# Declaring steps on different PSUM banks independent by part of a buffer instead of by whole buffer

## The chip, the cores and the metric

The kernel runs on one core of a Trainium2 chip. The metric is the device time of one execution in microseconds (us). A core has five engines that matter here, each with its own queue of instructions that it takes in order: PE (matrix products), DVE (elementwise work on vectors), ACT (activation functions and copies), POOL (elementwise work, without the accumulators) and SP (issues most DMAs). PE writes its results to PSUM, eight banks of 2 KB for each of 128 partitions; DVE and ACT read them from there. Engines wait for each other by semaphores.

## The reference

Two stages in one program. The first is a gated linear recurrence over 768 tokens for 4 batches of 8 heads of width 48, the second a feed-forward layer with the activation h * cos(h) on all 3072 tokens.

```python
f = 1.0 / (1.0 + np.exp(-f_logit))
for t in range(S):
    state = f[:, :, t, :, None] * state + np.einsum('bhd,bhe->bhde', k[:, :, t], v[:, :, t])
    y[:, :, t] = np.einsum('bhd,bhde->bhe', q[:, :, t], state)
x = np.ascontiguousarray(y.transpose(0, 2, 1, 3)).reshape(B * S, H * D)
h = x @ w_in                      # 384 -> 2048
out = (h * np.cos(h)) @ w_out     # 2048 -> 384
```

## The kernel before, in words

The tokens are cut into 12 pairs of two chunks of 128 tokens (three pairs a batch). For each pair n the recurrence is done in chunk form: the gates are made on ACT (steps ex, ln, fx, fy, lines 328 to 359), POOL and DVE scale queries and keys by the decays (qa, ka, qm, km, line 404 and before), PE makes running sums of log gates (cum, lines 374 and 380), products of queries and keys (sc, line 454; DVE masks them, am, line 458), and the products of keys and values for the carried state (ps, line 476; DVE adds the old state and scales, st at line 494 and sz at line 500). At last PE sums the outputs of the pair: y from masked products and values (`inner`, line 533) and yi from queries and carried state (`inter`, line 538), both with the matmul of line 528. The two chunks' outputs, py[0] and py[1], stand in one PSUM bank each.

The steps xe{n}.0 and xe{n}.1 (line 552) then copy the two banks to SBUF as bf16, each into its own half of one slot of the buffer x: `xg[g]` is a part of `x` (line 549). Which engine makes such a copy, ACT or DVE, is written down in the plan. The copies go through the helper of line 197, so the profile shows them as L197 with the tile x.

The feed-forward layer works in units of 128 or 256 tokens (13 units, `moe`, line 563). A unit of 256 tokens reads both halves of x: PE multiplies by w_in (h, line 576), ACT takes the cosine as a shifted sine from PSUM (co, line 581), DVE multiplies both into g (line 558), PE multiplies by w_out (o, line 592), ACT or DVE copies the result (ot) and a DMA stores it (out, line 603). The steps h{m} of unit m read x of pair m - 1 (units 0 and 1 both read pair 0).

The order of all steps is written out by hand in the table ORDER (line 36). A word such as `xe8.0:S1` names a step, its engine (T is PE, S is ACT, V is DVE, G is POOL, Y is SP) and the slots or banks that its new values get. `emit` (line 617) goes through the table and lets each step issue its instructions, so each engine's queue holds its steps in the order of the table. Semaphore waits are placed by the framework, which keeps instructions on one tile in order. PSUM is four tiles of two banks each (line 255), and for the framework a tile is one thing: instructions on its two banks are dependent unless told otherwise. That is what `apart` (line 642) does: it holds the last 12 steps on each PSUM tile (WITHIN, line 32) and declares a new step's instructions independent of an earlier step's on another engine if the steps touch no common bank and, by `places`, no common slot of any buffer in SBUF.

The two copies of a pair's x are such steps: their banks differ, but they lie in one tile in all pairs but the first, and both write the same slot of x. The words of the table for the pairs in which they stand on different engines of one tile: `xe1.0:V1 xe1.1:S`, `xe3.0:S1 xe2.1:S0 xe3.1:V xe2.0:V`, `xe6.1:S1 xe6.0:V`, `xe7.1:S0 xe7.0:V`, `xe8.0:S1 xe8.1:V`, `xe9.1:V2 xe9.0:S`, `xe11.0:V1 xe11.1:S`.

Of the kernel before, what the change touches and what calls it, by code (L numbers as in the profile page):

```python
# [616 lines left out]
def emit(tc, G, tiles):  # L617
    nc = tc.nc
    plan = []
    for word in ORDER.split():  # L620
        name, how = word.split(":")
        plan.append((G.steps[name], LETTER[how[0]], [int(x) for x in how[1:].split(",") if x]))
    assert len(plan) == len(G.steps)
    table, users = None, [[] for _ in tiles]
    for s, e, places in plan:
        for w in s.writes:
            v = w.whole
            if v.pool is not None and v.slot is None:
                v.slot = places.pop(0)
            w.first, w.final = not w.begun, w.left == 1  # L630
            w.begun, w.left = True, w.left - 1
        if s.table is not None:
            if s.table == "E" and table != "E":
                nc.scalar.preload_act_table_set("natural_log_exp_and_others")
            table = s.table
        n0 = nc.next_id()
        s.fn(e)
        made = (nc.find_inst_by_name(f"I-{i}") for i in range(n0 + 1, nc.next_id()))
        apart(tc, users, s, e, [i for i in made if i is not None])


def apart(tc, users, s, e, made):


    vals = [v.whole for v in s.reads + s.writes]
    banks = {b for v in vals if isinstance(v.pool, Banks) for b in range(v.slot, v.slot + v.pool.size)}
    places = {(v.pool.name, v.slot) for v in vals if v.pool is not None and not isinstance(v.pool, Banks)}
    for t in {b // 2 for b in banks}:
        for engine, others, theirs, there in users[t]:
            if engine != e and not banks & theirs and not places & there:  # L650
                for b in others:
                    for a in made:
                        tc.declare_no_dep(a, b, reason="the steps use different PSUM banks")
        users[t].append((e, made, banks, places))
        del users[t][:-WITHIN]


# [48 lines left out]
```

## Time and profile before

| what | value |
|---|---|
| median of 3 runs | 190.7 us (189.53 to 192.26) |
| the profiled execution | 189.83 us |
| its span, first to last instruction | 187.8 us |
| mean granted clock of PE | 0.991 |
| busy: PE, DVE, ACT, POOL | 175.9, 140.5, 134.4, 105.1 us |

The profile is that of one execution. A row of the timeline or of a group gives the start in us from the begin of the span, the length in us, the engine, the line of the kernel, the operation, what it writes and reads, and how many instructions are taken together; in square brackets stands the idle time of the engine just before, and what ended it. PEld is PE's loading of weights, which runs beside its matmuls. A row of the list of waits reads "who <- for whom: us in total, times, longest". In the rows of a tile the three numbers with slashes are the shortest, median and longest duration in ns. "The chain that ended last" is followed back from the last instruction, at each step to what released it. A merged row can overlap the next, since matmuls are pipelined and their ends are modelled.

### The profile page before, as it was taken

The page shows a single profiled execution, that of the slowest core. Times are in us where ns is not written, and L with a number is a line of the kernel's source. Part 1 is how long each engine was busy: PE and PEld are TensorE (multiplying, and loading weights), DVE is VectorE, ACT ScalarE, POOL GpSimd, SP SyncE. Part 2 cuts the span into 40 slices and gives each one's busy share as a digit, 9 for nine tenths or more (in the row PEclk, how much of TensorE's full clock was granted, in tenths as well). Part 3 has the DMA queues.
Part 4 walks back from the last instruction along what each step waited for, and adds up shares of the span by engine and source line. Part 5 has one row for each costly group of instructions (what it writes and reads, how often), then busy time and mean ns, then how long its engine had stood idle before and what let it go on. Part 6 is the DMA issues. An engine that isn't in the chain of part 4 may idle for free.

```text
span 187.8 us, 5973 instructions
## 1 busy us (share of the span) xinstructions
PE 175.9 (94%) x2540; PEld 125.8 (67%) x2540; DVE 140.5 (75%) x207; ACT 134.4 (72%) x193; POOL 105.1 (56%) x132
## 2 busy tenths in 40 slices
PE   7879877999999999999999999997999999999992
PEld 2345446886658876678767786665867876776661
DVE  5089869796697999999998889777999868335231
ACT  2798925997979999999999878688766573432310
POOL 3256787998548697998534979989960000000000
PEclk9999979999999999999999999999999999999999
DMA  5999999999927999976599997999581100111034
GB/s 126 268 198 266 365 358 324 280 291 251 268 43 197 231 289 186 266 186 128 108 205 256 263 248 135 171 254 224 131 196 43 47 0 0 45 42 42 0 129 168
DMA packets 72282, 33.94 MB, mean 181 GB/s; under 512 B 65344, under 2 KB 70720, under 8 KB 72256
## 3 DMA queue, kind: packets, MB, share of 16 engines
q1 hardware_dynamic: 68688, 32.09, 72.1%
q10 hardware_dynamic: 3568, 1.48, 3.3%
q8 instruction: 20, 0.33, 0.8%
q14 instruction: 6, 0.05, 0.1%
HBM read 25.17 MB, written 4.72 MB: 159 GB/s over the span
## 4 chain that ended last, share of the span: by engine, by line
PE 55%; DMA 11%; POOL 10%; ACT 9%; DVE 9%; issue 3%; SPq 1%; POOLq 0%; DVEq 0%; ACTq 0%
PE ps L592 24%; PE ps L576 23%; DMA f<-in_f_logit_dram 6%; POOL qk L404 4%; DMA k<-in_k_dram 3%; ACT co L581 3%; PE ps L454 3%; PE ps L528 3%; DVE am L458 3%; DMA out_dram<-ot 2%; POOL vb L197 2%; DVE qk L404 2%; POOL sp L363 2%; POOL vt L197 2%; DVE sz L500 2%
## 5 line engine op out<-in xcount | busy, mean ns | idle before, releaser
L558 DVE TENSOR_TENSOR g<-ps,co 128x1024 bf16<-128x1024 f32 x48 | 60.8, 1308 | 16.7 <-ACT co L581 16.0
L576 PE MATMUL ps<-x,w_in_bf 128*128 128x256 bf16 (+1 forms) x624 | 68.8, 266 | 3.0 <-ACT x L197 1.3
L581 ACT ACTIVATE co<-ps,halfpi 128x1024 bf16<-128x1024 f32 x48 | 52.3, 1115 | 23.6 <-PE ps L576 22.4
L592 PE MATMUL ps<-w_out_bf,g 128*128 128x384 bf16 x384 | 68.2, 326 | 0.0
L576 PEld LDWEIGHTS <-w_in_bf 128*128 128x128 bf16 x624 | 57.0, 99 | 11.9 <-issue 3.5
L592 PEld LDWEIGHTS <-g 128*128 128x128 bf16 x384 | 36.3, 98 | 21.3
L458 DVE TENSOR_TENSOR am<-ps,pmask 128x1024 bf16<-128x1024 f32 x24 | 28.9, 1219 | 6.0 <-PE ps L454 5.6
L404 POOL TENSOR_TENSOR qk<-k,bi 128x384 bf16<-128x384 f32 x22 | 21.9, 1003 | 0.9
L404 POOL TENSOR_TENSOR qk<-q,b 128x384 bf16<-128x384 f32 x21 | 20.8, 1000 | 1.0 <-ACT b L395 0.3
L363 POOL TENSOR_TENSOR sp<-ls 128x384 bf16<-128x384 f32 x10 | 10.0, 1000 | 13.2 <-ACT ls L333 10.5
L264 PE MATMUL ps<-zero 128*128 128x512 bf16 x50 | 14.9, 432 | 1.2 <-DVE zero L203 1.2
L197 POOL COPY vt<-vb 64x384 bf16<-64x384 bf16 x28 | 14.2, 509 | 1.9 <-ACT vb L197 0.5
L500 DVE TENSOR_TENSOR sz<-ps,b 64x192 bf16<-64x192 f32 x40 | 14.1, 354 | 1.2
L351 POOL TENSOR_TENSOR k<-k,f 128x384 f32<-128x384 f32 (+1 forms) x12 | 11.2, 932 | 5.2 <-DMA k<-in_k_dram 4.3
L494 DVE TENSOR_TENSOR ps<-ps,sz 64x192 f32<-64x192 f32 x32 | 11.7, 365 | 1.7 <-PE ps L476 0.7
L329 ACT ACTIVATE f<-f 128x768 f32<-128x768 f32 (+1 forms) x14 | 10.3, 746 | 2.8 <-DMA f<-in_f_logit_dram 2.2
L197 ACT COPY ot<-ps 128x384 f32<-128x384 f32 (+1 forms) x13 | 5.6, 438 | 8.3 <-PE ps L592 4.2
L197 DVE COPY ot<-ps 128x384 f32<-128x384 f32 (+1 forms) x13 | 6.8, 532 | 6.2 <-PE ps L592 2.9
L197 POOL CAST vb<-v 128x768 bf16<-128x768 f32 x9 | 7.3, 823 | 7.2 <-DMA v<-in_v_dram 7.2
L341 POOL TENSOR_TENSOR q<-f,q 128x384 f32<-128x384 f32 x10 | 9.9, 999 | 1.7 <-DMA q<-in_q_dram 1.5
L454 PE MATMUL ps<-qkt 48*64 48x128 bf16 x384 | 9.9, 225 | 0.5 <-DVE qkt L197 0.2
L197 ACT COPY vt<-vb 64x384 bf16<-64x384 bf16 x20 | 10.0, 507 | 0.3
(64 smaller groups left out, 167.1 us busy)
## 6 DMA issues: line engine op xcount, KB each, us to landing
out_dram<-ot SPq DMA_DIRECT2D x22, 192.0 KB, 2.3
f<-in_f_logit_dram SPq DMA_DIRECT2D x10, 384.0 KB, 5.9
v<-in_v_dram SPq DMA_DIRECT2D x10, 384.0 KB, 6.1
q<-in_q_dram SPq DMA_DIRECT2D x10, 384.0 KB, 5.3
k<-in_k_dram SPq DMA_DIRECT2D x10, 384.0 KB, 6.5
g<-in_moe_w_in_dram SPq DMA_DIRECT2D x4, 768.0 KB, 9.1
g<-in_moe_w_out_dram SPq DMA_DIRECT2D x4, 768.0 KB, 7.1
v<-in_v_dram ACTq DMA_DIRECT2D x2, 384.0 KB, 5.9
```

The lines of the kernel that those rows point to most:

```text
L197: (nc.scalar.copy if e == "ACT" else eng(e).tensor_copy)(out=o, in_=i)
L264: G.step(f"zf{i}", ("PE",), lambda e, dump=dump: nc.tensor.matmul(dump.ap, lhsT=zero[:, 0:128], rhs=zero, start=True, stop=True), writes=[ ...
L363: G.step(f"ad{n}", ("POOL",), lambda e: eng(e).tensor_add(out=sp.ap[:, 0, :, 0:D], in0=soft.ap[:, :, 0, :], in1=soft.ap[:, :, 1, :]), read ...
L404: G.step(f"{nm}{n}.{u}", ("POOL", "DVE") if cut else ("POOL",), lambda e, u=u, j=j, src=src, dec=dec: eng(e).tensor_mul(out=qkp[u][j].ap[: ...
L454: nc.tensor.matmul(o[t, r, 2 * a + g, :].rearrange("p (e n) -> p e n", e=2), lhsT=qkv(u)[s, 1, a, g, x, :], rhs=qkv(u)[s, 0, a, g, :, :], ...
L458: G.step(f"am{n}.{u}", ("DVE",), lambda e, u=u, sc=sc: nc.vector.tensor_mul(out=am[u].ap.rearrange("p r b n -> p (r b) n"), in0=sc.ap.rear ...
L494: nc.vector.tensor_add(out=view()[s], in0=view()[s], in1=S0.ap[s, :, r, :])
L500: eng(e).tensor_mul(out=new.ap[s, :, r, :].rearrange("p (u a) n -> p u a n", u=2), in0=view()[s].rearrange("p (u a) n -> p u a n", u=2), i ...
L558: nc.vector.tensor_mul(out=o.rearrange("p b (n e) -> p b e n", e=2), in0=ph.ap.rearrange("p (b e n) -> p b e n", e=2, n=64), in1=co.ap.rea ...
L576: nc.tensor.matmul(ph.ap[:, i * T:(i + 1) * T].rearrange("p (g t) -> p g t", t=C), lhsT=w_in_bf[:, kk, f0:f0 + 128], rhs=xa[:, :, kk, :], ...
L581: G.step(f"co{m}.{j}", ("ACT",), lambda e, ph=ph, co=co: nc.scalar.activation(out=co.ap, in_=ph.ap, func=AF.Sin, bias=halfpi), reads=[ph], ...
L592: nc.tensor.matmul(po.ap[:, 0:DM], lhsT=gT.ap[:, j, i * C:(i + 1) * C], rhs=w_out_bf[:, j, :], start=(po.first and j == 4 * s), stop=(po.f ...
```

## The change

Only `apart` is changed. In place of the set of slots that a step touches, it keeps for each value outside PSUM the value as named by the step (a whole or a part), the whole behind it, and if it is written. Two steps meet if one of them writes, both use the same slot of the same pool, and the values are in each other's way: different wholes in one slot (an old and a new occupant), the same part, or one of them the whole. Two different parts of one whole do not meet, nor do two reads. Steps on different banks that don't meet are declared independent.

```diff
-    places = {(v.pool.name, v.slot) for v in vals if v.pool is not None and not isinstance(v.pool, Banks)}
+    home = lambda v: v.whole.pool is not None and not isinstance(v.whole.pool, Banks)
+    uses = [(v, v.whole, i) for i, vs in enumerate((s.reads, s.writes)) for v in vs if home(v)]
+
+    def meet(theirs):
+        for v, w, wr in uses:
+            for v2, w2, wr2 in theirs:
+                if (wr or wr2) and w.pool is w2.pool and w.slot == w2.slot:
+                    if w is not w2 or v is v2 or v is w or v2 is w2:
+                        return True
+        return False
     for t in {b // 2 for b in banks}:
         for engine, others, theirs, there in users[t]:
-            if engine != e and not banks & theirs and not places & there:
+            if engine != e and not banks & theirs and not meet(there):
                 for b in others:
                     for a in made:
                         tc.declare_no_dep(a, b, reason="the steps use different PSUM banks")
-        users[t].append((e, made, banks, places))
+        users[t].append((e, made, banks, uses))
```

## The prediction

> **What bounds the kernel now.** I read the page first (busy shares, the slices, the shares of the chain that ended last), then the list of who waited for whom, then the rows of the tile x, and last the timeline around each copy that the change touches.
>
> ```profile
> span 187.8 us, 5973 instructions
> PE 175.9 (94%) x2540; PEld 125.8 (67%) x2540; DVE 140.5 (75%) x207; ACT 134.4 (72%) x193; POOL 105.1 (56%) x132
> ...
> PEclk9999979999999999999999999999999999999999
> DMA  5999999999927999976599997999581100111034
> ...
> PE 55%; DMA 11%; POOL 10%; ACT 9%; DVE 9%; issue 3%; SPq 1%; POOLq 0%; DVEq 0%; ACTq 0%
> ```
>
> PE is busy for 94% of the span at nearly full clock, and the chain that ended last runs mostly over PE. The DMA engines are full in most slices of the first three quarters, so POOL, which prepares each pair from loaded data, can hold PE up as well. From the list of waits, the rows that join the copies of x with anything:
>
> ```profile
> DVE x L197 <- ACT x L197: 3.3, 4, 1.6
> ACT x L197 <- DVE x L197: 3.1, 3, 1.7
> ...
> PE ps L576 <- ACT x L197: 1.3, 1, 1.3
> PE ps L576 <- DVE x L197: 1.0, 2, 0.6
> ...
> PE ps L576 <- DVE sz L500: 0.7, 2, 0.4
> ```
>
> Seven times the copy of one half of x on one of DVE and ACT waits for the copy of the other half on the other, 3.3 + 3.1 = 6.4 us together. PE stands at its first matmul of line 576 behind such a copy three times, 1.3 + 1.0 = 2.3 us. These 2.3 us, and whatever stands behind them, are all that the edit can give directly.
>
> ```profile
> L197 ACT CAST x<-ps x13: 478/478/485, 20.2 to 149.6; 128x384 bf16<-128x384 f32 x13
> L197 DVE CAST x<-ps x11: 539/558/558, 22.4 to 149.0; 128x384 bf16<-128x384 f32 x11
> ```
>
> **What changes.** Both built programs hold the same instructions in the same order on each engine; only waits differ. The halves xg[0] and xg[1] read two banks of one PSUM tile and write two parts of one slot of x. Before, the common slot kept them dependent; after, the parts are disjoint and the wait between them goes. That happens in pairs 1, 2, 3, 6, 7, 8, 9 and 11, where the steps xe stand on different engines. Pairs 4, 5 and 10 have both copies on one engine, and pair 0 has its two banks in different tiles. In return each copy waits for its own PE sums; and PE's first line-576 step after such a pair, which waited once (for the later copy), now waits twice: DVE's copy at the weight load, ACT's at the matmul. A few copies of line 197 and activations of line 581 also name DVE or PE work that they had covered through the other copy. That work has long ended when they are reached, so I take nothing for it.
>
> **Pair 1 (31 to 33 us).**
>
> ```profile
> 31.21 0.51 PE L528 MATMUL ps<-qkt,sz 128*32 128x128 bf16 x24
> ...
> 31.65 0.10 PEld L576 LDWEIGHTS <-w_in_bf 128*128 128x128 bf16 x1
> 31.92 0.54 DVE L197 CAST x<-ps 128x384 bf16<-128x384 f32 x1
> ...
> 32.49 0.48 ACT L197 CAST x<-ps 128x384 bf16<-128x384 f32 x1 [0.51 <-DVE x L197]
> ...
> 33.02 4.09 PE L576 MATMUL ps<-x,w_in_bf 128*128 128x256 bf16 x36 [1.30 <-ACT x L197]
> ```
>
> ACT is free from 32.49 - 0.51 = 31.98, and the sums end at 31.72. So ACT copies from 32.0 to 32.48 beside DVE (31.92 to 32.46). PE's weight load, done ahead at 31.65 before, now waits for DVE and takes 0.10 after it; the matmul starts at about 32.60 instead of 33.02. Gain 0.42. ACT goes on to its weight cast 0.5 us sooner; the activations behind it move with PE.
>
> The Trainium skill, TensorE: Matmul & The Clock Gate, section "Step-by-step: what each phase is for", says that PE draws weight loads ahead of matmuls still in flight. The trace agrees in the load at 31.65, 1.37 us ahead of its matmul. By that page's column rule a load that is not overlapped costs an estimated 128 / 1.2 = 107 ns, which speaks against this edit: eight loads would give back 0.85 us.
>
> By the row, eight loads would cost 8 x 0.10 = 0.8 us if PE stood idle at all eight. It stands idle at three, and at two of these ACT's copy ends last, so I charge it once, above.
>
> **Pair 6 (104 to 106 us).**
>
> ```profile
> 105.16 0.48 ACT L197 CAST x<-ps 128x384 bf16<-128x384 f32 x1
> 105.27 0.62 PE L528 MATMUL ps<-am,vt 128*32 128x128 bf16 x32
> 105.67 0.56 DVE L197 CAST x<-ps 128x384 bf16<-128x384 f32 x1 [0.89 <-ACT x L197]
> ...
> 106.28 8.02 PE L576 MATMUL ps<-x,w_in_bf 128*128 128x256 bf16 x72 [0.39 <-DVE x L197]
> ...
> 112.69 0.82 POOL L197 CAST vb<-v 128x768 bf16<-128x768 f32 x1 [1.22 <-DMA v<-in_v_dram]
> ...
> 115.21 1.96 POOL L404 TENSOR_TENSOR qk<-k,bi 128x384 bf16<-128x384 f32 x2
> 117.48 0.50 PE L476 MATMUL ps<-vb,qk 64*64 64x48 bf16 x28
> ```
>
> DVE's copy moves into its 0.89 us of waiting and is done before ACT's ends at 105.64; PE's own sums of pair 7 end at 105.89. So PE goes on at 105.89, 0.39 sooner. But at 117.48 PE takes ps9.1, which needs POOL's products, done at 115.21 + 1.96 = 117.17, and POOL had stood 1.22 us for a load of v. If that load lands when it did, only 117.48 - 117.17 = 0.31, less 0.04 for the signal (the step from the end of ACT's copy in pair 1, 32.97, to PE's start is 0.05), gets past this point: 0.27. The 0.42 of pair 1 must pass there too. Together the two are worth between 0 and 0.42 + 0.39 = 0.81; I take 0.27, since the load of v is the nearest row that decides it.
>
> **Pair 8 (126 to 131 us).**
>
> ```profile
> 125.99 0.51 PE L528 MATMUL ps<-qkt,sz 128*32 128x128 bf16 x24
> 126.83 0.31 PE L476 MATMUL ps<-vb,qk 64*64 64x48 bf16 x16
> 127.40 0.48 ACT L197 CAST x<-ps 128x384 bf16<-128x384 f32 x1
> 127.91 0.56 DVE L197 CAST x<-ps 128x384 bf16<-128x384 f32 x1 [1.57 <-ACT x L197]
> 128.38 0.35 DVE L494 TENSOR_TENSOR ps<-ps,sz 64x192 f32<-64x192 f32 x1
> 128.52 1.47 PE L576 MATMUL ps<-x,w_in_bf 128*128 128x256 bf16 x12 [0.62 <-DVE x L197]
> 128.65 1.21 DVE L458 TENSOR_TENSOR am<-ps,pmask 128x1024 bf16<-128x1024 f32 x1
> 129.92 0.63 PE L528 MATMUL ps<-am,vt 128*32 128x128 bf16 x32
> 130.30 0.74 DVE L500 TENSOR_TENSOR sz<-ps,b 64x192 bf16<-64x192 f32 x2
> 131.10 5.59 PE L576 MATMUL ps<-x,w_in_bf 128*128 128x256 bf16 x48 [0.38 <-DVE sz L500]
> ```
>
> ACT reaches its half late (127.40) and DVE, idle for 1.57 us, queued the carry st10, the mask am9.1 and the states sz10 behind its own. After, DVE copies once the sums end (126.50): 126.54 to 127.10. The carry needs ps10 (end 127.14): 127.18 instead of 128.38, 1.20 sooner, and am9.1 and sz10 with it (am9.1 ends at 128.66, sz10 at 131.04 - 1.20 = 129.84). PE starts h8.01 when ACT's copy ends, 127.88 + 0.04 = 127.92, not 128.52: 0.60. It is at y9 at 129.92 - 0.60 = 129.32, where am9.1 is ready, and reaches h8.30 at 131.10 - 0.38 - 0.60 = 130.12, where sz10 is ready too: the 0.38 goes as well. Gain 0.98, with 0.60 as its lower end, if something else takes the place of sz10.
>
> **The other pairs.**
>
> ```profile
> 57.87 0.56 DVE L197 CAST x<-ps 128x384 bf16<-128x384 f32 x1 [0.53 <-ACT x L197]
> 58.75 0.56 DVE L197 CAST x<-ps 128x384 bf16<-128x384 f32 x1 [0.33 <-ACT x L197]
> ...
> 132.07 0.48 ACT L197 CAST x<-ps 128x384 bf16<-128x384 f32 x1 [0.93 <-DVE x L197]
> ...
> 149.63 0.48 ACT L197 CAST x<-ps 128x384 bf16<-128x384 f32 x1 [1.70 <-DVE x L197]
> ```
> ```profile
> 58.54 7.97 PE ps L576 x72
> ...
> 175.19 9.11 PE ps L592 x56
> ```
>
> In pairs 2, 3, 9 and 11 a copy moves forward by up to 0.9 us, but PE is busy over all of them (58.54 to 66.51; 131.10 to 136.69; in pair 11 with the next unit's matmuls), so I take nothing. Without that cover each would give at most a copy, 0.5 us. Pair 7 shows no wait.
>
> **The sum.** 0.27 + 0.98 = 1.25 us, bounds 0.60 and 0.42 + 0.39 + 0.98 = 1.79. From 131 us to the output matmuls at 175.19 and on, PE has no listed idle, so what is won there should reach the end. The profiled execution took 189.83 us (span 187.8 and 2.0 around it), which gives 188.6. The median of the runs shown, 190.7, lies 0.9 above it and gives 189.45. I predict between them, 189.0.
>
> **Rivals.**
> 1. *The waits come back elsewhere.* PE gets to y9, to h8.30 or to ps9.1 sooner and stands there for POOL or a load. For it: full DMA slices and POOL's 1.22 us behind v. Against: the rows at 130.12 above, where the operands are ready. Worth 0 to 0.5, so about 190.4.
> 2. *Everything moves along*, the load of v too, since its issue hangs on POOL and SP work that hangs on PE: the full 1.79, about 188.4 against the middle of the two bases. Removing even all 2.3 us of waits listed stays below 2%.
> 3. *Slower: the weight loads.* If a load with a wait on it stops PE at all eight places, also where PE is not idle, that costs 0.8 us; it decides once less than 0.8 of the 1.25 is won. With the gain of rival 1 at nothing the time is 190.7 + 0.8 = 191.5. Against: DVE's copy has ended when PE comes to the load in pairs 2, 3, 7, 9 and 11.
> 4. *The two copies slow each other*, reading one PSUM tile at once. If each takes the sum, 0.48 + 0.56 = 1.04 us, nothing is won: 190.7. The trace has no such pair to show it; ACT's copy took 478 to 485 ns in all 13 cases, in some beside DVE reading another tile.
>
> The Trainium skill, PSUM — Partial Sum Buffer, section "Specifications (TRN2)", says that the two engines read PSUM in parallel at full speed where the banks differ. No run here shows that for one tile.
>
> That the edit does nothing is excluded by the differing waits.
>
> **Chances and range.** Forecast 0.60, everything moves along 0.12, waits come back 0.16, slower by the loads 0.08, copies slow each other 0.04. Two per cent, 3.8 us, is about what a measurement of this kernel can tell from no change: the runs before alone spread over 2.7 us. No case reaches it by its own arithmetic; leaving room for a timing effect that I do not see (loads that fall differently), I say 0.07 faster, 0.88 within, 0.05 slower. The range goes from the lowest run before less the upper bound, 189.53 - 1.79 = 187.7, a little lowered to 187.4, up to the slower rival, 191.5.
>
> **What would show it.** Right: no wait between ACT x and DVE x in the list; PE's idle at 33.02 down to about 0.9, those of pairs 6 and 8 gone, and that on sz10 gone; DVE's carry st10 straight after the sums of pair 8 and 10, some 1.2 us sooner than before. Wrong: a new PE idle time at 117 or 129 to 131 of the size of the gain, copies of x longer than 0.56 us, or weight loads of line 576 with idle time at the other pairs.

## The result, and the profile after

The changed kernel takes 188.7 us at the median of 21 runs (186.57 to 190.19), the kernel before 190.74 (188.65 to 192.53, 21 runs). The ratio is 0.9867, 95% interval 0.9839 to 0.9896: faster, by 2.0 us at the medians and by 2.0 to 3.1 us by the interval, and so by less than 2%. The ratio leaves out the slow runs of each kernel, those more than 1.5% above its fastest, which are 7 of the 21 of the changed kernel; so it shows more than the medians do. Forecast were 189.0 and no change over 2%.

In the profiled execution (189.68 us) PE's clock was low for longer in the first 31 us than in the profile before, as the clock row shows, so its span hardly shows the gain, and I compare stretches after that point instead. From its page:

```profile
span 187.5 us, 5972 instructions
PE 177.0 (94%) x2536; PEld 126.9 (68%) x2540; DVE 140.4 (75%) x207; ACT 134.3 (72%) x193; POOL 105.3 (56%) x132
...
PEclk9999957999999999999999999999999999999999
```

From the list of waits and the rows of the tile x of the same execution:

```profile
DVE x L197 <- PE ps L528: 1.8, 4, 0.6
ACT x L197 <- PE ps L528: 1.7, 3, 1.1
...
PEld L576 <- DVE x L197: 0.8, 1, 0.8
...
PE ps L576 <- ACT x L197: 0.7, 1, 0.7
```
```profile
L197 ACT CAST x<-ps x13: 470/478/486, 20.0 to 148.9; 128x384 bf16<-128x384 f32 x13
L197 DVE CAST x<-ps x11: 534/557/558, 22.5 to 148.9; 128x384 bf16<-128x384 f32 x11
```

The copies of x no longer wait for each other; they wait for PE's sums, as they should. Of PE's three waits for a copy at line 576 one is left, that of pair 1. The copies take as long as before, though they now run side by side on two banks of one tile. The timeline at the three places of the prediction:

```profile
32.33 0.51 PE L528 MATMUL ps<-qkt,sz 128*32 128x128 bf16 x24
32.89 0.56 DVE L197 CAST x<-ps 128x384 bf16<-128x384 f32 x1 [0.55 <-PE ps L528]
32.99 0.47 ACT L197 CAST x<-ps 128x384 bf16<-128x384 f32 x1
...
33.50 0.55 PEld L576 LDWEIGHTS <-w_in_bf 128*128 128x128 bf16 x6 [0.84 <-DVE x L197]
33.51 0.71 PE L576 MATMUL ps<-x,w_in_bf 128*128 128x256 bf16 x5 [0.68 <-ACT x L197]
```
```profile
105.97 0.56 DVE L197 CAST x<-ps 128x384 bf16<-128x384 f32 x1
...
106.36 0.48 ACT L197 CAST x<-ps 128x384 bf16<-128x384 f32 x1
...
107.02 1.70 PE L576 MATMUL ps<-x,w_in_bf 128*128 128x256 bf16 x14
```
```profile
118.56 0.50 PE L476 MATMUL ps<-vb,qk 64*64 64x48 bf16 x28 [0.25 <-POOL qk L404]
```
```profile
127.06 0.51 PE L528 MATMUL ps<-qkt,sz 128*32 128x128 bf16 x24
127.62 0.56 DVE L197 CAST x<-ps 128x384 bf16<-128x384 f32 x1 [0.21 <-PE ps L528]
...
128.33 0.36 DVE L494 TENSOR_TENSOR ps<-ps,sz 64x192 f32<-64x192 f32 x1
128.47 0.48 ACT L197 CAST x<-ps 128x384 bf16<-128x384 f32 x1
...
129.00 1.47 PE L576 MATMUL ps<-x,w_in_bf 128*128 128x256 bf16 x12
...
131.13 3.12 PE L576 MATMUL ps<-x,w_in_bf 128*128 128x256 bf16 x27
```

In pair 1 PE's idle falls from 1.30 to 0.68 us. In pair 6 and ahead of unit 8 the brackets are gone, and so is that on sz10. A new wait has come at ps9.1 (118.56), on POOL's qk, at the place that the prediction named. From the start of the sums yi8 to that of h8.30 it was 131.10 - 125.99 = 5.11 us before and is 131.13 - 127.06 = 4.07 now.

**The whole span in stretches.** ACT has the same instructions in the same order, all of them recorded, in every kernel here but the two that move a copy of pair 8. So I cut each execution at the starts of seven of them (before: co at 30.86, the load of a function table at 45.79, x at 105.16, co at 112.08, fx at 121.21, vt at 126.87, co at 136.73 us) and subtract. The stretch from 121.21 to 126.87 is 5.66 us in all of them and is left out. Below, `all` is the change once more; the other names are those of the experiments.

| execution | up to 30.86 | 31 to 46 (pair 1) | 46 to 105 | pair 6 | ps9.1 | pairs 8, 9 | to the end |
|---|---|---|---|---|---|---|---|
| before | 30.86 | 14.92 | 59.38 | 6.92 | 9.13 | 9.86 | 51.03 |
| base_look1 | 30.57 | 14.96 | 60.15 | 6.92 | 9.13 | 9.86 | 50.95 |
| base_look2 | 30.31 | 14.89 | 59.77 | 6.92 | 9.13 | 9.85 | 50.94 |
| only8 | 30.54 | 14.82 | 60.27 | 6.92 | 9.13 | 8.74 | 50.93 |
| rest | 30.44 | 14.80 | 59.30 | 6.92 | 9.13 | 9.77 | 50.84 |
| only1 | 29.45 | 14.40 | 59.59 | 6.92 | 9.14 | 9.85 | 50.94 |
| only1_look1 | 31.65 | 14.31 | 60.29 | 6.92 | 9.13 | 9.86 | 50.94 |
| only1_look2 | 29.66 | 14.40 | 59.37 | 6.91 | 9.13 | 9.85 | 50.94 |
| only16 | 29.52 | 14.39 | 59.96 | 6.47 | 9.44 | 9.85 | 50.94 |
| all | 30.64 | 14.40 | 59.99 | 6.47 | 9.37 | 8.74 | 51.07 |
| changed kernel | 31.98 | 14.30 | 60.08 | 6.47 | 9.45 | 8.75 | 50.83 |
| all_v8 | 29.78 | 14.40 | 60.00 | 6.47 | 9.13 | 8.73 | 50.86 |

Against the kernel before, the change wins 0.5 us at pair 1 (14.80 to 14.96 without the rule there, 14.30 to 14.40 with it), 0.45 at pair 6, of which it gives back 0.24 to 0.32 at ps9.1, and 1.12 at pairs 8 and 9. The first and third stretches vary from execution to execution whatever the kernel, by 2.5 and 1.0 us.

### The profile page after: what moved, and what is told of

It reads as the page before. It is cut to its first block, busy times and chain, and to the rows that moved or that the text cites. A ratio compares the mean times of both kernels' runs of the same rounds, so it can differ in the third digit from the quotient of the medians.

```text
span 187.5 us, 5972 instructions
## 1 busy us (share of the span) xinstructions
PE 177.0 (94%) x2536; PEld 126.9 (68%) x2540; DVE 140.4 (75%) x207; ACT 134.3 (72%) x193; POOL 105.3 (56%) x132
## 4 chain that ended last, share of the span: by engine, by line
PE 47%; DMA 15%; POOL 14%; ACT 8%; issue 8%; DVE 4%; SPq 2%; POOLq 0%
PE ps L592 22%; PE ps L576 18%; DMA k<-in_k_dram 9%; POOL qk L404 6%; DMA f<-in_f_logit_dram 6%; PE ps L454 3%; ACT co L581 2%; POOL sp L363 2%; POOL vb L197 2%; POOL k L351 2%; PE ps L528 2%; DVE qk L404 2%; POOL q L341 1%; SPq L296 1%; PE ps L476 1%
## 5 line engine op out<-in xcount | busy, mean ns | idle before, releaser
L576 PE MATMUL ps<-x,w_in_bf 128*128 128x256 bf16 (+1 forms) x624 | 69.6, 269 | 1.0 <-ACT x L197 0.7
L264 PE MATMUL ps<-zero 128*128 128x512 bf16 x46 | 14.7, 451 | 1.5 <-DVE zero L203 1.2
```

Of the source, the lines that this page charges most:

```text
L264: G.step(f"zf{i}", ("PE",), lambda e, dump=dump: nc.tensor.matmul(dump.ap, lhsT=zero[:, 0:128], rhs=zero, start=True, stop=True), writes=[ ...
L576: nc.tensor.matmul(ph.ap[:, i * T:(i + 1) * T].rearrange("p (g t) -> p g t", t=C), lhsT=w_in_bf[:, kk, f0:f0 + 128], rhs=xa[:, :, kk, :], ...
```

## The experiments

**Which pairs the gain comes from.** Three kernels have the finer rule for some pairs alone, a fourth for all. The edit, on the changed kernel (`places` and `held` are the old set of slots, of this step and of the earlier one):

```diff
+FINE = (8,)
...
+    fine = s.name.startswith("xe") and int(s.name[2:-2]) in FINE
...
-            if engine != e and not banks & theirs and not meet(there):
+            if engine != e and not banks & theirs and not (meet(there) if fine else places & held):
```

FINE is (8,) in only8, (1, 6) in only16, (2, 3, 7, 9, 11) in rest, and every pair in all. Line numbers stand one higher than before. Expected of only8:

> The finer rule for the copies of pair 8 alone. Prediction's step: 0.98 us less than before (0.62 us of PE idle ahead of unit 8's first matmul and 0.38 us ahead of h8.30 go), ratio about 0.995. Rival 1 (waits come back): 0 to 0.5 less. Rival 3 (loads): 0.1 more than the first at most.

Measured: 188.59 us against 190.45, ratio 0.9943 (0.9907 to 0.9978), that is 0.4 to 1.8 us less. (The medians are 1.86 apart. In the nine runs of each kernel whose mean granted clock is 0.987 to 0.991 they are 1.05 apart.)

```profile
126.46 0.51 PE L529 MATMUL ps<-qkt,sz 128*32 128x128 bf16 x24
127.02 0.56 DVE L198 CAST x<-ps 128x384 bf16<-128x384 f32 x1 [0.21 <-PE ps L529]
...
128.40 1.47 PE L577 MATMUL ps<-x,w_in_bf 128*128 128x256 bf16 x12
...
130.53 3.65 PE L577 MATMUL ps<-x,w_in_bf 128*128 128x256 bf16 x31
```

From yi8 to h8.30 it is 130.53 - 126.46 = 4.07 us, 1.04 less than before, and both idle times are gone. In the table the stretch loses 9.86 - 8.74 = 1.12. The step of the prediction (0.98) holds, and rival 1 does not at this place.

Expected of only16:

> The finer rule for pairs 1 and 6 alone. Prediction's step: 0.27 us less than before, since POOL's products for pair 9, behind the load of v, hold PE at ps9.1; a new PE wait on POOL's qk there. Rival 2 (everything moves along): 0.81 less and no such wait.

Measured: 189.69 against 190.45, ratio 0.9954 (0.9916 to 0.9992). PE's idle times in its timeline:

```profile
31.23 4.10 PE L577 MATMUL ps<-x,w_in_bf 128*128 128x256 bf16 x36 [0.86 <-DVE x L198]
...
116.05 0.50 PE L477 MATMUL ps<-vb,qk 64*64 64x48 bf16 x28 [0.24 <-POOL qk L405]
127.08 1.47 PE L577 MATMUL ps<-x,w_in_bf 128*128 128x256 bf16 x12 [0.62 <-DVE x L198]
```

The wait on POOL's qk at ps9.1 is there, so the mechanism is shown. The size is less plain: the table shows 0.45 at pair 6 less 0.31 at ps9.1, 0.14 net, and pair 1's 0.5 beside it, which this experiment does not tell apart. Together that is 0.64, between the 0.27 of the prediction's step and the 0.81 of rival 2.

Expected of rest:

> The finer rule for pairs 2, 3, 7, 9 and 11 alone, where PE was busy over the copies. Prediction's step: no change, within 0.1 us. Rival 3 (a weight load with a wait on it stops PE): 0.5 us more. If the whole change gives more than 1.8 us because these pairs help too: 0.5 or more less.

Measured: 189.72 against 190.45, ratio 0.9975 (0.9939 to 1.0011): no difference can be told, and 0.5 us more is outside the interval (0.2 more to 1.2 less). Its timeline has, where before a row of the same 48 matmuls took 5.59 us:

```profile
130.47 5.51 PE L577 MATMUL ps<-x,w_in_bf 128*128 128x256 bf16 x48 [0.38 <-DVE sz L501]
```

That is the 0.09 of the stretch of pairs 8 and 9: a stall of less than 0.1 us stood inside a merged row that I had read as PE busy. In only8, which keeps the old rule at pair 9, the 48 matmuls take 5.51 us too, so either rule removes this stall and the two gains don't add. Rival 3 falls here: the weight loads of five pairs have a wait on them and no loss can be seen.

Expected of all:

> The whole change, through the same switch as the three others, all pairs on. Prediction: 1.25 us less than before, and the sum of the three parts. The runs of the change gave 2 us less; if the parts are additive and the steps right, the parts' sum shows which of them is mis-sized.

Measured: 188.11 against 190.45, ratio 0.9881 (0.983 to 0.9932). In the table the parts stand side by side: pairs 1 and 6 as in only16, pairs 8 and 9 as in only8, and ps9.1 takes back 0.24.

**What the gain of pair 8 is made of.** Two kernels keep the old rule and move one copy in the table of the order (only the changed words of the line are shown):

```diff
-xe8.0:S1 xe8.1:V
+xe8.0:S1 xe8.1:S
```
```diff
-xe8.0:S1 xe8.1:V
+xe8.0:V1 xe8.1:V
```

The first is both8_act. Expected:

> The rule of before; the copy of pair 8 that DVE made goes to ACT, behind ACT's own, so DVE no longer waits for ACT there and PE still waits for ACT. If the gain of pair 8 is two things, DVE's queue and PE's wait for the second copy: PE's 0.62 us ahead of h8.01 shrinks by about 0.2 only (two copies on ACT took 0.86 us in a row, 0.48 + 0.56 apart before), and the 0.38 us ahead of h8.30 goes since sz10 is early: 0.6 less. If DVE's queue is all of it: 1.0 less. If only the wait for the copy counts: 0.2 less.

Measured: 188.97 against 189.82, ratio 0.9948 (0.9915 to 0.9981).

```profile
126.04 0.51 PE L528 MATMUL ps<-qkt,sz 128*32 128x128 bf16 x24
...
127.31 0.36 DVE L494 TENSOR_TENSOR ps<-ps,sz 64x192 f32<-64x192 f32 x1 [0.92 <-ACT vt L197]
127.44 0.86 ACT L197 CAST x<-ps 128x384 bf16<-128x384 f32 x2
...
128.35 1.47 PE L576 MATMUL ps<-x,w_in_bf 128*128 128x256 bf16 x12 [0.40 <-ACT x L197]
...
130.48 3.78 PE L576 MATMUL ps<-x,w_in_bf 128*128 128x256 bf16 x33
```

The idle ahead of h8.01 falls from 0.62 to 0.40 only, and that on sz10 is gone: 130.48 - 126.04 = 4.44, 0.67 less than 5.11. DVE's carry starts at 127.31, though ACT has not copied yet. So the gain of pair 8 is two things, and DVE's queue is one of them; 0.6 was expected for that case.

The second is both8_dve. Expected:

> The rule of before; both copies of pair 8 on DVE, which is free from 126.3 us on, so that the late ACT has no part in them. DVE copies from 126.54 to about 127.65 and PE does not wait ahead of h8.01 (0.62 us gone); the carry st10 and sz10 come 0.56 us later than with the finer rule, and 0 to 0.3 us of idle stay ahead of h8.30: 0.7 to 1.0 less than before. If the gain needs the finer rule itself: nothing.

Measured: 189.33 against 189.82, ratio 0.9954 (0.9923 to 0.9985).

```profile
126.53 0.51 PE L528 MATMUL ps<-qkt,sz 128*32 128x128 bf16 x24
...
127.09 1.02 DVE L197 CAST x<-ps 128x384 bf16<-128x384 f32 x2 [0.21 <-PE ps L528]
...
128.28 1.47 PE L576 MATMUL ps<-x,w_in_bf 128*128 128x256 bf16 x12
...
130.74 3.52 PE L576 MATMUL ps<-x,w_in_bf 128*128 128x256 bf16 x29 [0.26 <-DVE sz L500]
```

Now unit 8 starts without idle and 0.26 stays ahead of h8.30: 130.74 - 126.53 = 4.21, 0.90 less. So the two idle times answer to two causes that can be moved one by one, and most of the gain is to be had without the rule, by taking the copy off the late engine.

**What takes back pair 6's gain.** On top of the whole change, SP's order of loads (parts of two lines of the table):

```diff
-q9:Y0 q8:Y1 k9:Y2 k10:Y0
+q9:Y0 q8:Y1 k9:Y2
...
-v9:Y2 v8:Y0
+v8:Y0 v9:Y2 k10:Y0
```

> The whole change, and on SP's queue the load of v for pairs 8 and 9 issued ahead of the load of k for pair 10. If the load of v for pair 8, through POOL's qk, is what takes back 0.3 us of pair 6's gain at ps9.1 (PE idle of 0.17 to 0.25 us there), that idle goes and the time is 0.25 less than with the change alone. If PE waits there for something else: the idle stays and the time is that of the change.

Measured: 187.65 against 189.82, ratio 0.9886 (0.9841 to 0.9931). The times alone don't separate it from the change (0.983 to 0.9932 in all); the traces do. In all, and then in all_v8, POOL and PE at ps9.1:

```profile
112.62 0.82 POOL L198 CAST vb<-v 128x768 bf16<-128x768 f32 x1 [1.43 <-DMA v<-in_v_dram]
...
117.15 0.50 PE L477 MATMUL ps<-vb,qk 64*64 64x48 bf16 x28 [0.17 <-POOL qk L405]
```
```profile
110.20 0.83 POOL L198 CAST vb<-v 128x768 bf16<-128x768 f32 x1
...
116.06 0.50 PE L477 MATMUL ps<-vb,qk 64*64 64x48 bf16 x28
```

POOL's wait of 1.43 us for the load and PE's behind it are both gone, and the stretch of ps9.1 is back at 9.13 us. So it was the load of v. By the table this version gains 0.24 us more than `all`.

**Whether pair 1's gain reaches the end.**

> The finer rule for pair 1 alone, one look. The prediction took it that pair 1's 0.42 us has to pass ps9.1 at 117 us and is cut there: PE idle of 0.1 us or more behind POOL's qk at ps9.1, the idle of pairs 6 and 8 as before, and about 0.3 us of gain there. If the loads are issued sooner as well, since their issue hangs on work that hangs on PE: no idle at ps9.1, and all of 0.42 us reaches the end.

FINE is (1,). Measured, one run of 188.03 us:

```profile
31.18 4.11 PE L577 MATMUL ps<-x,w_in_bf 128*128 128x256 bf16 x36 [0.87 <-DVE x L198]
...
104.57 8.02 PE L577 MATMUL ps<-x,w_in_bf 128*128 128x256 bf16 x72 [0.39 <-DVE x L198]
126.81 1.47 PE L577 MATMUL ps<-x,w_in_bf 128*128 128x256 bf16 x12 [0.62 <-DVE x L198]
129.38 5.59 PE L577 MATMUL ps<-x,w_in_bf 128*128 128x256 bf16 x48 [0.38 <-DVE sz L501]
```

There is no idle at ps9.1 (9.14 in the table), and what follows is as before. Pair 1's gain is not cut there: by then POOL and its loads are sooner by as much. The load of v for pair 8 is issued at 105.38 us in the kernel before and at 103.74 here, 0.22 and 0.30 behind ACT's copy of pair 6. So its issue comes some 70 us after pair 1 and moves along with it, and it comes ahead of the place where PE gains at pair 6 (106.28 before).

That leaves the stretch from 36 to 105 us, where POOL waits for the load of v of pair 4 in some executions. Four more executions, two of the kernel before and two of only1, were to tell whether pair 1's gain goes into that wait.

> The kernel before once more, for the stretch from ACT's cosine at 36.24 us to its copy of x at 105.16 us, in which POOL waits for the load of v of pair 4 in some executions and not in others. If that wait comes by chance: 68.9 to 69.8 us, as in the kernels without the finer rule for pair 1 so far. If it comes from pair 1's gain, since the load lands at its own time: 68.9, with no wait.

> The same as the look before it, a second execution: by chance 68.9 to 69.8 us; if the wait comes from pair 1's gain 68.9.

> The finer rule for pair 1 alone, the same stretch. If the wait for the load of v comes by chance: 68.9 to 69.8 us, no longer on the mean than without the rule. If pair 1's gain is given back there: 69.2 to 69.7 every time, some 0.4 longer than the kernel before.

> The same as the look before it, a second execution: by chance 68.9 to 69.8 us; if pair 1's gain is given back, 69.2 to 69.7.

Measured, one run each: 190.28, 189.55, 190.97 and 188.13 us. The rows of POOL in base_look1 and in only1_look2:

```profile
67.36 0.82 POOL L198 CAST vb<-v 128x768 bf16<-128x768 f32 x1 [0.89 <-DMA v<-in_v_dram]
```
```profile
64.88 0.83 POOL L199 CAST vb<-v 128x768 bf16<-128x768 f32 x1
```

The wait is there without the rule and missing with it, so the rule does not make it (line numbers are shifted by a line or two here). From 36.24 to 105.16, the stretch of the expectations, the five executions without the rule for pair 1 in the table take 68.85 to 69.82 us (mean 69.32), the seven with it 69.02 to 69.85 (mean 69.52). Part of the 0.2 between the means is ACT's own lead at 36.24, which it loses again by 45.79; from there on the means are 59.78 and 59.90. With ranges that overlap this far, the means alone can't tell whether some of pair 1's 0.5 us is given back.

The traces tell more. The load is issued 14.4 to 14.5 us behind the start of the stretch from 46 to 105 us in the five executions without the rule, and 14.4 to 14.7 in the seven with it. So its issue moves along with pair 1's gain. What varies is its time from issue to landing, 5.7 to 7.4 us without the rule and 6.2 to 7.4 with it, and POOL's wait varies with that. Where POOL has no wait, this stretch takes 59.30 and 59.38 us without the rule and 59.37 with it. Nothing shows that pair 1's gain is given back; why the landing varies stays open.

## Why the prediction was right

- *What bounds the kernel.* Right. In the stretches of pairs 1, 6 and 8 the time falls by what PE no longer stands idle, to 0.1 us. The stretch left out of the table is the same in all executions, and the last one differs by 0.24 at most, with no order by kernel.
- *Pair 1.* Right: 0.42 forecast. PE's idle ahead of its first matmul of line 576 there is 1.17 to 1.33 us in the five executions without the rule and 0.68 to 0.87 in the seven with it, 0.44 less on the mean; the stretch gives 0.5 (mean 14.88 without the rule, 14.37 with it), and where the rest of that comes from is not shown. One term was too large: I had charged 0.10 us for a weight load that waits for DVE, and the last section shows it at 0.01.
- *The cap at ps9.1.* Right for pair 6, wrong for pair 1. The wait came, at the place and for the reason named, and took back 0.24 to 0.32 of 0.45. But "the 0.42 of pair 1 must pass there too" failed: a gain made 80 us ahead moves the issue of the load along, as only1 shows. The step that put both gains under one cap is the one that failed. I took 0.27 for both pairs; the table gives 0.51 + 0.45 - 0.28 = 0.68 (0.28 is the middle of 0.24 and 0.32). That term was the one most off, by 0.41.
- *Pair 8.* Right in both parts: 0.98 forecast, 1.04 to h8.30, and 1.12 with the stall of 0.08 at pair 9, which goes with it. The copies on one engine show the two parts apart.
- *The other pairs.* Right within 0.1 us in the traces; "PE is busy over all of them" hid a stall of 0.08 us at pair 9.
- *The sum.* 1.25 forecast, bounds 0.60 and 1.79. The stretches give 0.68 + 1.12 = 1.8, which is the upper bound, the medians 2.0, the ratio 2.0 to 3.1. What the times show beyond the stretches goes at least in part with the clock. Among the runs of `all` and the 29 runs of the kernel before taken beside them, those of like mean clock are 1.8 us apart (0.979 to 0.982), 1.4 (0.987 to 0.991) and 2.0 (0.998 and over), though `all` has only one, three and two such runs. In the lowest group stand 16 of the 29 runs before and one of the six of `all`, and that puts the medians 2.3 apart. Why the clock is low in more runs of one than of the other is not shown.
- *Luck.* The 189.0 came within 0.3 us of 188.7 because two errors partly cancel. It took a base of about 190.3, half way between the profiled execution and the median of three runs, where the 21 runs give 190.74; and it took a gain of 1.25 where the medians show 2.0.
- *Small slips.* The signal at ps9.1 is taken at 0.04 beside a row that gives 0.05, and rival 2 comes to 188.5 from the middle of the two bases, not 188.4; neither changes the forecast. A measurement tells more than the 2% that was thought: the interval of 21 runs each is 0.6% wide.
- *The rivals.* The copies do not slow each other (470 to 486 ns side by side). The weight loads cost nothing that the runs show. Waits came back, but by 0.3 us. Of the rivals, the one in which everything moves along came nearest in size. Its mechanism holds for pair 1 and not for pair 6, with which the load of v did not move.

## What to carry to other kernels

A wait between two short copies costs more than a copy when one of the engines comes late: price what is queued behind the waiting engine, not only the next matmul. Here a gain passed a load when it was made before the load was issued (pair 1), and was cut there when it was made after (pair 6); so look up when the load that could cut a gain is issued. And dependence that is tracked per tile or slot should be told apart by part before any order is tuned, since an order made by hand can't show a wait that the framework adds.

## What the runs showed of the hardware

- A weight load that has to wait for a semaphore did not delay its matmul. In all, DVE's copy ends at 31.77 + 0.54 = 32.31, the load starts at 32.36 and the matmul at 32.37, 0.06 us after the copy. It was 0.05 us in pair 1 before, where the load stood ready more than a microsecond ahead:

```profile
31.77 0.54 DVE L198 CAST x<-ps 128x384 bf16<-128x384 f32 x1
32.36 1.64 PEld L577 LDWEIGHTS <-w_in_bf 128*128 128x128 bf16 x16 [1.04 <-DVE x L198]
32.37 1.81 PE L577 MATMUL ps<-x,w_in_bf 128*128 128x256 bf16 x15 [0.87 <-DVE x L198]
```

- Two copies in a row on one engine overlap: 0.86 us on ACT where one takes 0.48 (both8_act), 1.02 on DVE where one takes 0.56 (both8_dve).
- The stretch up to 30.86 us goes with PE's granted clock, and varies most among the executions of the table. With no dip in the clock row up to there it took 29.45 to 29.66 us in three executions and 29.78 in a fourth; with one short dip, 30.31 to 30.86; in the two with the longest, 31.65 and 31.98.
